# An attention and feed-forward kernel: three batch-1 transposes placed later, four start-up loads merged into two

## The chip, the cores and the metric

The kernel runs on one core of a Trainium2 chip. The metric is device time in microseconds (us). The profile covers one execution; the times come from six. Five engines are named as in the profile: PE is the matmul engine (PEld its weight loads), DVE the vector engine, ACT the scalar engine, POOL GpSimd, and SP the engine that here only issues transfers. Each runs its own instruction stream in program order and waits on the others through semaphores.

## The reference

Squared-ReLU attention over 8 batches, 12 heads, 448 tokens and 64 features a head, and then a feed-forward block on the joined heads (768 wide, 3072 inside) with a layer norm ahead of it and a residual:

```python
scores = scale * np.matmul(q, k.transpose(0, 1, 3, 2))
attn = np.maximum(scores, 0.0) ** 2 / S
x = np.matmul(attn, v)                       # heads joined: (8, 448, 768)
...
xn = (x - mu) / np.sqrt(var + 1e-06) * g_ln
out = x + np.maximum(xn @ w_ch1, 0.0) @ w_ch2
```

## The kernel before

**Units.** Heads go in pairs: a batch has six, and pair i is pair i % 6 of batch i // 6, so pairs 0 to 5 are batch 0, 6 to 11 batch 1, 12 to 17 batch 2. A pair's scores are made by `att_QK` in four tiles of keys (three of 128 keys, and the last 64 keys, which two pairs share), ReLU is done by ACT or DVE on the way out of PSUM, DVE squares in `att_square`, and `att_AV` multiplies with v and writes the transposed x (`xT_of(b, pair)`) as bf16.

**Two ways of getting q and k transposed.** Pairs 0 to 11 are loaded whole into `early` (`load_heads`) and transposed on PE against an identity (`pe_T`, line 235). From pair 12 on, `load_qk` fills one of three slots of `qk_ring` by three loads on POOL's queue (lines 174 to 176), and `att_T` issues one DMA transpose of that slot on SP's queue (line 259) into one of three `qkT` buffers. So the transpose of pair 16 needs the load of pair 16 landed, and the buffer of pair 13 read for the last time; its landing frees the slot for the load of pair 19.

**Batch 0.** Its attention runs alone at the start (`step_fine`, `first_end`), fed by loads whose order is written out by hand in the last part of the kernel. All loads that cast float32 to bf16 go through POOL's queue in program order: batch 0's heads, batch 1's, the first weights `w1` in six pieces, the second weights `w2` in four, and then pairs 12 to 14. Batch 0's q and k came in groups of heads 2-3, 4-5, 6-7 and 8-11 (heads 0 and 1 through two other queues). The v of heads 0 to 3 and the last 64 rows of all v stood between the groups 4-5 and 6-7.

**From then on a batch's first feed-forward product carries the next batch's attention.** `ffn_1_all(b)` walks over 24 column tiles ni of 128; each is 12 matmuls at line 446 and one ReLU on ACT. At chosen ni (`IN_SECOND` = 3, 6, 9, 13, 15, 18, 21 for b = 1) an `excursion` puts three score tiles of the next batch in between; when it holds a pair's last tile, `queued` issues the transpose of the pair three further on and notes the load six further on, which goes out at the next excursion. The order in batch 1 is: ni = 3: pair 12, first three tiles; ni = 6: pair 12's last tile, pair 13 (then the transpose of 15 is issued); ni = 9: pair 13's third tile, pair 14 (transpose of 16); ni = 13 (transpose of 17); ni = 15: two tiles of pair 15 and the first of pair 16, whose halves go to spare PSUM banks and are cleared by ACT and DVE.

**The residual and the statistics.** `ffn_x(b, ki)` transposes one of six 128-feature pieces of x to token order by a DMA transpose on SP's queue (line 423) into `x_tok`. For batch 1 pieces 0 to 2 go out during batch 0's second product and pieces 3 to 5 in `ffn_1_all(1)`. `ffn_stats` (lines 437 to 439, DVE, two bn_stats and one bn_aggr) reads a 128-token tile of all six pieces; `STATS_AT[b]` gives the ni at which the four tiles of the batch are done. The results are used in `ffn_rstd`, after the last ni.

Of the kernel before, what the change touches and what calls it, by code (L numbers as in the profile page):

```python
# [11 lines left out]
def kernel(  # L12
# [17 lines left out]
    B, H, S, D = q.shape  # L30
# [108 lines left out]
    def v_parts(b):  # L139
        v_sb = v1_sb if b == 1 else v_ring  # L140
        return (v_sb[:, :H * NF * D].rearrange("p (h e) -> p h e", h=H),
                v_sb[:, H * NF * D:].rearrange("p (a e) -> p a e", a=NPAIR))

    def load_heads(b, pieces):
        v_heads, v_rest = v_parts(b)
        for name, h0, hs in pieces:
            heads = slice(h0, h0 + hs)
            if name == "q":
                nc.gpsimd.dma_start(first_q[b][:, heads].rearrange("p h j d -> p h (j d)"),  # L149
                                    q[b, heads].rearrange("h (p j) d -> p h (j d)", j=NJ))  # L150
            elif name == "k":
                nc.gpsimd.dma_start(first_k[b][:, heads, :NF].rearrange("p h t d -> p h (t d)"),  # L152
                                    k[b, heads, :SF].rearrange("h (p t) d -> p h (t d)", t=NF))
            elif name == "k last":
                nc.gpsimd.dma_start(first_k[b][:SS, heads, NF], k[b, heads, SF:].rearrange("h s d -> s h d"))
            elif name == "v":
                nc.gpsimd.dma_start(v_heads[:, heads], v[b, heads, :SF].rearrange("h (p t) d -> p h (t d)", t=NF))
            elif name == "v last":
                for e in range(4):
                    r0 = row0(e // 2, e % 2)  # L160
                    nc.gpsimd.dma_start(v_rest[r0:r0 + SS, e // 2::2, r0:r0 + D],
                                        v[b, e::4, SF:].rearrange("g s d -> s g d"))

    def row0(i, hh):

        return D * ((i + hh) % 2)
# [246 lines left out]
    def tiles_of(b):  # L413
        return range(b * S // P, (b + 1) * S // P)
# [10 lines left out]
    def x_carry(b):  # L425

        nc.scalar.copy(xT[:, :, :D], x_first[:, :, S - D:] if b == 0 else xT[:, :, S:])
# [291 lines left out]
    def flush_loads():  # L719
        while loads:  # L720
            load_qk(loads.pop(0))
# [103 lines left out]
    def ffn_1_first():  # L825
        f_ps, m_ps = next_f(), next_f()
        tiles = [t[:, :S] for t in (f_ps, m_ps, spare[1], next_sc()[:, 0])]
        for ki in range(K1):
            if ki < GAIN_FIRST:
                center_part(ki, mean0)  # L830
            else:
                nc.vector.tensor_tensor(xc[:, ki, :], mean0, xT_of(0, ki), op=Alu.add)
                nc.scalar.activation(xc[:, ki, :], xc[:, ki, :], Act.Identity, scale=g_sb[:, ki:ki + 1])
            for ni, ps in enumerate(tiles):
                nc.tensor.matmul(ps, w1[:, ki, ni * P:(ni + 1) * P], xc[:, ki, :],
                                 start=(ki == 0), stop=(ki == K1 - 1))
        for ni, ps in enumerate(tiles):
            nc.scalar.activation(h[:, ni, CARRY:], ps, Act.Relu)
        for t in range(2):
            att_square(NPAIR, t)  # L840
        excursion(1)
# [4 lines left out]
    T_IN_FIRST = {10: 3, 13: 4, 16: 5}  # L846
    X_AT = (9, 10, 11, 12, 13, 14)
    V_AT = {22: PE_T * NPAIR + 2, 23: PE_T * NPAIR + 4}
    STATS_AT = {0: (18, 21, 23), 1: (14, 16, 19, 22), 2: (2, 5, 8, 14), 3: (2, 5, 8, 11)}
    IN_SECOND = (3, 6, 9, 13, 15, 18, 21)  # L850
    IN_REST = (1, 3, 6, 9, 12, 15, 18)
    X_SUMS_AT = {0: (0, 1, 2), 4: (3,), 7: (4,)}
# [1 line left out]
    def ffn_1_all(b):  # L854
        ms = tiles_of(b)
        units = () if b < UNIT_FROM else (UNIT,) if b < B - 1 else (*LAST_UNITS, UNIT)
        for ni in range(NI0 if b == 0 else 0, units[0] if units else K2):
            if b == 0 and ni == NI0:
                ffn_1_first()
            if b == 0 and ni == NI0 + 2:  # L860
                x_carry(0)
            if b == 0 and ni == X_AT[0]:

                nc.sync.dma_start(held, h[:1, ni - 1, CARRY:CARRY + 16])
            if b == 0 and ni in X_AT:
                ffn_x(b, X_AT.index(ni))
            if b == 0 and ni == IN_FIRST[-1] + 1:
                flush_loads()
            if b == 0 and ni in V_AT:
                load_v(V_AT[ni])  # L870
            bursts = (IN_FIRST, IN_SECOND, IN_REST)[min(b, 2)]

            late = ni == 0 and b > 1 and b * S // (2 * P) - (b - 1) * S // (2 * P) == 1
            ffn_1(ni, spare[1] if late or b < B - 1 and ni in bursts and len(ready) > 1 else None)
            flush()
            at = STATS_AT[min(b, 2) if b < B - 1 else 3][:len(ms)]
            if ni in at:
                ffn_stats(ms[at.index(ni)])
            if b >= UNIT_FROM:
                for n in X_SUMS_AT.get(ni, ()):  # L880
                    x_sum(n)
            if b == 1:
                for n, part in enumerate(p for p, at in zip(LATE_SUMS, SUMS_AT) if at == ni):
                    if ni == REST_AT and n < 2:
                        ffn_2_first_rest(n)
                    w2_sums(*part)
            if b == 0:
                if ni in IN_FIRST:
                    excursion(3)
                if ni == IN_FIRST[-1] + 3:  # L890
                    next_AV(bank=spare[1])
                if ni in T_IN_FIRST:
                    att_T(NPAIR + T_IN_FIRST[ni])
            elif b < B - 1:
                if ni in bursts:
                    first = nc.vector if b > 1 and ni == bursts[0] else nc.scalar
                    excursion(3, third=(first, nc.vector), **(dict(evac_by=nc.scalar) if b == 1 else {}))
                    if b == 1 and ni == bursts[1]:
                        for ki in range(X_FIRST, K1):
                            ffn_x(1, ki)  # L900
                    while ni > bursts[3] and held_stores:
                        held_stores.pop(0)()
                if b == 1 and ni == K2 - 1:
                    flush_loads()
                    next_AV(bank=spare[1])

        late = []

        def between(n):
            if n == 2:  # L910
                flush_loads()
            if n == 3:
                next_AV(bank=sc_turn.items[0][:, 0], evac_by=nc.scalar, later=late)
            if n == 5:
                posts.extend(late)


        f0, f1 = f_turn.items
        if b == B - 1:
            unit(units[0], (f0, spare[1], spare[0], f1), accs[0], accs[2])  # L920
            unit(units[1], (f1, f0, spare[1], spare[0]), accs[3], accs[4])
            unit(units[2], (spare[0], f1, f0, spare[1]), accs[0], accs[2])
        elif units:
            unit(UNIT, (f0, spare[1], spare[0], f1), accs[0], accs[1], between)
# [84 lines left out]
    with tc.manual_schedule(engines=set(ENGINES)):  # L1009
        load_early()  # L1010
        load_heads(0, [("q", 2, 2), ("k", 2, 2)])
        make_identity(nc, identity)
        load_heads(0, [("k last", 0, 4), ("q", 4, 2), ("k", 4, 2), ("k last", 4, 4), ("v", 0, 4),
                       ("v last", 0, H), ("q", 6, 2), ("k", 6, 2), ("q", 8, 4), ("k", 8, 4),
                       ("k last", 8, 4), ("v", 4, 4), ("v", 8, 4)])
        load_heads(1, [("q", 0, 2), ("k", 0, 2), ("k last", 0, H)])
        load_heads(1, [("q", 2, 4), ("k", 2, 4)])
        load_w1(0)
        load_w1(1)
        load_w1(2)  # L1020
        load_heads(1, [("q", 6, 6), ("k", 6, 6), ("v", 0, H), ("v last", 0, H)])
        for c in range(3, NCH):
            load_w1(c)
        warm_up(20)
        att_T(0)
        warm_up(2)
        for i in range(0, NPAIR, 2):
            step_fine(i)
        first_end()
        load_w2(B11, 0, 0)  # L1030
        load_w2(B21, 1, 0)
        load_w2(B12, 0, 1)
        load_w2(B22, 1, 1)
        nc.gpsimd.memset(qk_ring, 0.0)
        i = PE_T * NPAIR
        load_qk(i)
        load_qk(i + 1)
        load_qk(i + 2)
        load_v(i)
        for b in range(B):  # L1040
            ffn_1_all(b)
            if b == 0:
                ffn_2_first()
            else:
                ffn_2_all(b)
        flush()
# [30 lines left out]
```

## Time and profile before

| | |
|---|---|
| median of 6 runs | 518.68 us (517.47 to 519.88) |
| the profiled execution | 519.27 us, span 517.5 us |
| PE busy | 508.9 us, 98% of the span |
| DVE, ACT, POOL busy | 403.1, 287.3, 225.7 us |
| PE clock granted | full over the span |
| share of the chain that ended last | PE 80%, DMA 14%, POOL 4% |
| POOL's transfer queue | 25.75 MB |

The span is what the profiler saw of the program; the execution's own time is 1.8 us more. PE is busy nearly throughout, so the time of the kernel is PE's work and the few moments when PE waits. A wait of PE is printed in its timeline in square brackets behind the instruction that it precedes, with what ended it.

### The profile page before, as it was taken

The numbers are of one execution on the slowest core, as the hardware profiler recorded it, in microseconds if no ns is written. First come the engines' busy times: TensorE is split into PE (matmuls) and PEld (weight loads), VectorE is DVE, ScalarE is ACT, GpSimd is POOL, SyncE is SP. The second block draws the span as 40 slices with busy tenths as digits, with TensorE's granted clock in tenths as the row PEclk, the third lists the DMA queues.
The fourth block names the chain that finished last, engine by engine and source line by source line (L and its number), as shares of the span: only waits on it lengthen the run. The fifth ranks groups of instructions, "written<-read, shape, count | busy, mean of one in ns | idle before, by whom it ended". The sixth has DMA issues, their size and how long they took to land.

```text
span 517.5 us, 14362 instructions
## 1 busy us (share of the span) xinstructions
PE 508.9 (98%) x5979; PEld 321.6 (62%) x5979; DVE 403.1 (78%) x720; ACT 287.3 (56%) x487; POOL 225.7 (44%) x259
## 2 busy tenths in 40 slices
PE   8899999999999999999999999999999999999996
PEld 4345566546875576655766557655766557667865
DVE  5866779969988779687785868987896869993855
ACT  6887551777238772387723876487624876234220
POOL 9817113967732863228532376337632000330031
PEclk9999999999999999999999999999999999999999
DMA  9999999999636991559924599469934300250022
GB/s 114 174 202 198 183 204 159 142 154 183 82 83 103 117 107 49 124 75 131 92 52 109 80 123 140 81 81 112 83 69 111 65 1 3 72 114 3 1 60 64
DMA packets 175312, 53.05 MB, mean 103 GB/s; under 512 B 154256, under 2 KB 175248, under 8 KB 175248
## 3 DMA queue, kind: packets, MB, share of 16 engines
q0 software_dynamic: 103744, 25.75, 55.7%
q1 hardware_dynamic: 70976, 26.03, 26.8%
q8 instruction: 46, 0.75, 0.6%
q10 hardware_dynamic: 528, 0.37, 0.2%
q14 instruction: 18, 0.15, 0.1%
HBM read 51.91 MB, written 11.01 MB: 122 GB/s over the span
## 4 chain that ended last, share of the span: by engine, by line
PE 80%; DMA 14%; POOL 4%; issue 1%; ACT 1%; DVE 0%; SPq 0%; POOLq 0%
PE f L521 34%; PE f L446 29%; PE f L672 6%; DMA qk_ring<-in_k_dram 6%; DMA s_sb<-in_v_dram 4%; PE f L330 4%; PE sc L300 3%; DMA qkT_t<-qk_ring 2%; PE f L300 1%; DMA w<-in_k_dram 1%; PE sc L295 1%; PE sc L330 1%; POOL w L152 1%; PE f L353 1%; POOL w L213 1%; POOL w L149 1%
## 5 line engine op out<-in xcount | busy, mean ns | idle before, releaser
L446 PE MATMUL f<-xc,w 128*64 128x448 bf16 x1872 | 189.0, 354 | 0.1
L446 PEld LDWEIGHTS <-w 128*64 128x64 bf16 x1872 | 105.1, 110 | 76.6 <-issue 14.4
L521 PE MATMUL f<-w,s_sb 128*64 128x384 bf16 (+2 forms) x1584 | 130.0, 324 | 0.0
L448 ACT ACTIVATE h<-f 128x448 bf16<-128x448 f32 x156 | 85.9, 551 | 65.7 <-PE f L446 60.9
L521 PEld LDWEIGHTS <-s_sb 128*64 128x64 bf16 x1584 | 92.3, 110 | 34.8
L310 ACT ACTIVATE at<-sc 128x896 bf16<-128x896 f32 x120 | 103.1, 919 | 10.1 <-PE sc L300 10.1
L313 DVE TENSOR_TENSOR at<-at 128x896 bf16<-128x896 bf16 x168 | 96.6, 620 | 6.8 <-ACT at L310 6.0
L554 POOL TENSOR_TENSOR o_t<-o_t,x_tok 128x384 f32<-128x384 f32 x26 | 25.3, 972 | 148.1 <-ACT o_t L553 148.1
L174 POOL DMA_DIRECT2D qk_ring<-in_q_dram x36 | 46.8, 1301 | 85.6 <-DMA qkT_t<-qk_ring 60.0
L553 ACT ACTIVATE o_t<-f,rstd 128x384 f32<-128x384 f32 x26 | 15.1, 581 | 95.8 <-DVE acc_t L558 37.0
L515 DVE TENSOR_TENSOR s_sb<-h 128x1536 bf16<-128x1536 bf16 x65 | 64.4, 1004 | 0.0
L175 POOL DMA_DIRECT2D qk_ring<-in_k_dram x36 | 55.9, 1554 | 10.8 <-DMA w<-in_moe_w_ch_dram 10.8
L521 PE MATMUL f<-w,h 128*64 128x384 bf16 x624 | 52.9, 326 | 0.0
L176 POOL DMA_DIRECT2D qk_ring<-in_k_dram x36 | 46.6, 1295 | 5.3 <-DMA w<-in_moe_w_ch_dram 4.8
L306 DVE TENSOR_SCALAR at<-f 128x448 bf16<-128x448 f32 x59 | 35.5, 615 | 13.8 <-PE f L300 13.8
L521 PEld LDWEIGHTS <-h 128*64 128x64 bf16 x624 | 36.5, 110 | 13.6
L554 POOL TENSOR_TENSOR acc_t<-acc_t,x_tok 128x384 f32<-128x384 f32 x24 | 28.5, 1195 | 20.0 <-ACT acc_t L553 19.9
L186 POOL DMA_DIRECT2D v_ring<-in_v_dram x36 | 33.3, 1268 | 0.0
L330 PE MATMUL f<-at,v_ring 128*64 128x448 bf16 x248 | 31.1, 357 | 0.5 <-DMA v_ring<-in_v_dram 0.5
L410 DVE SCALAR_TENSOR_TENSOR xc<-f,g_sb,xc 128x448 bf16<-128x448 f32 x45 | 28.5, 678 | 3.8 <-PE f L404 3.8
L300 PE MATMUL sc<-qkT_t 64*128 64x448 bf16 x192 | 30.0, 357 | 0.5 <-DMA qkT_t<-qk_ring 0.5
L369 DVE TENSOR_SCALAR xT<-f 128x448 bf16<-128x448 f32 x22 | 13.6, 618 | 18.9 <-ACT at L310 11.1
(130 smaller groups left out, 566.1 us busy)
## 6 DMA issues: line engine op xcount, KB each, us to landing
w<-in_moe_w_ch_dram POOLq DMA_DIRECT2D x6, 768.0 KB, 13.5
w<-in_moe_w_ch_dram POOLq DMA_DIRECT2D x4, 1152.0 KB, 29.1
v_ring<-in_v_dram POOLq DMA_DIRECT2D x21, 192.0 KB, 4.8
qk_ring<-in_q_dram POOLq DMA_DIRECT2D x36, 112.0 KB, 5.0
qk_ring<-in_k_dram POOLq DMA_DIRECT2D x36, 96.0 KB, 4.9
out_dram<-o_t SPq DMA_DIRECT2D x8, 168.0 KB, 2.2
out_dram<-acc_t SPq DMA_DIRECT2D x7, 168.0 KB, 2.2
out_dram<-o_t SPq DMA_DIRECT2D x8, 144.0 KB, 2.1
```

What stands on the lines that cost most here:

```text
L174: nc.gpsimd.dma_start(q_to, q[b, heads].rearrange("x (p j) d -> p j x d", j=NJ))
L175: nc.gpsimd.dma_start(k_to[:, :NF], k[b, heads, :SF].rearrange("x (p t) d -> p t x d", t=NF))
L176: nc.gpsimd.dma_start(k_to[:SS, NF], k[b, 2 * a:2 * a + 2, SF:].rearrange("x s d -> s x d"))
L300: nc.tensor.matmul(by_j(half[hh]), k_of(i, r, t, P), q_of(i, r), start=True, stop=True)
L310: nc.scalar.activation(at, ps[:, :, :S], Act.Relu)
L313: nc.vector.tensor_mul(attn[i, t], attn[i, t], attn[i, t])
L330: nc.tensor.matmul(ps[hh * D:(hh + 1) * D, :], weights, values, start=start, stop=stop)
L446: nc.tensor.matmul(ps[c * D:(c + 1) * D, :], w1[:, ki, n0:n0 + D], xc[:, ki, :], start=(ki == 0), stop=(ki == K1 - 1))
L448: nc.scalar.activation(h[:, ni, CARRY:], ps, Act.Relu)
L515: nc.vector.tensor_tensor(s_sb[:, n], x, y, op=op)
L521: nc.tensor.matmul(ps[c * D:(c + 1) * D, :d1 - d0], stat[:, ki, c * D:(c + 1) * D], w2[:, slot, ki, d0:d1], start=(start and ki == 0), sto ...
L554: nc.gpsimd.tensor_tensor(o_t, o_t, x_half(m, dh), op=Alu.add)
```

## The change

Three statements are edited. In batch 0's list of loads, q of heads 4 and 5 and q of heads 6 and 7 become one load at the place of the former, and likewise k. In batch 1, pieces 3 to 5 of x go out one excursion later, at ni = 9, so on SP's queue they stand behind the transpose of pair 16 instead of ahead of it; and the statistics of batch 1 stand at ni = 16, 18, 20, 22 instead of 14, 16, 19, 22.

```diff
-    STATS_AT = {0: (18, 21, 23), 1: (14, 16, 19, 22), 2: (2, 5, 8, 14), 3: (2, 5, 8, 11)}
+    STATS_AT = {0: (18, 21, 23), 1: (16, 18, 20, 22), 2: (2, 5, 8, 14), 3: (2, 5, 8, 11)}
...
-                    if b == 1 and ni == bursts[1]:
+                    if b == 1 and ni == bursts[2]:
                         for ki in range(X_FIRST, K1):
                             ffn_x(1, ki)
...
         load_heads(0, [("q", 2, 2), ("k", 2, 2)])
         make_identity(nc, identity)
-        load_heads(0, [("k last", 0, 4), ("q", 4, 2), ("k", 4, 2), ("k last", 4, 4), ("v", 0, 4),
-                       ("v last", 0, H), ("q", 6, 2), ("k", 6, 2), ("q", 8, 4), ("k", 8, 4),
-                       ("k last", 8, 4), ("v", 4, 4), ("v", 8, 4)])
+        load_heads(0, [("k last", 0, 4), ("q", 4, 4), ("k", 4, 4), ("k last", 4, 4), ("v", 0, 4),
+                       ("v last", 0, H), ("q", 8, 4), ("k", 8, 4), ("k last", 8, 4), ("v", 4, 4), ("v", 8, 4)])
```

## The prediction

> **What bounds the kernel now.** I read PE's timeline first, for its brackets: PE is busy 98% of the span, so only its waits can be won. After 1.23 us it waits five times, and never after 110.12 us. The four larger ones:
>
> ```profile
> 13.88 0.76 PE L235 MATMUL f<-identity,w 112*64 112x112 bf16 x16 [1.18 <-DMA w<-in_q_dram]
> ...
> 18.82 0.57 PE L330 MATMUL f<-at,v_ring 128*64 128x448 bf16 x4 [0.49 <-DMA v_ring<-in_v_dram]
> ...
> 90.03 0.55 PE L300 MATMUL sc<-qkT_t 64*128 64x448 bf16 x4 [0.47 <-DMA qkT_t<-qk_ring]
> ...
> 110.12 0.36 PE L300 MATMUL f<-qkT_t 64*128 64x448 bf16 x2 [0.68 <-DMA qkT_t<-qk_ring]
> ```
>
> The first is pair 3's PE transpose, late by q of heads 6 and 7. The second is pair 2's product with v. The third is pair 12, the first that comes through the ring. The fourth is the first tile of pair 16, at ni = 15. All are waits for transfers, 2.82 us together. As PE then runs on without a gap, what is won at 110 us reaches the end whole.
>
> Next the chain that ended last: it comes to 90 us not over PE but over transfers.
>
> ```profile
> 52.41 31.80 DMA qk_ring<-in_k_dram
> 84.36 5.63 DMA qkT_t<-qk_ring
> ```
>
> The last load of pair 12 lay 31.8 us in POOL's queue behind w1 and w2. So the start-up gains nothing beyond 0.47 us unless this stream of loads ends earlier too. Whether it can is in the stretches (windows; last two columns DMA share and GB/s) and in POOL's timeline:
>
> ```profile
> 4.00:9.00 5.00, 5.00 (x54) 2.88 (x52) 2.73 (x9) 2.56 (x5) 5.00 (x9) 1.00 1.25 125
> 9.00:14.00 5.00, 3.82 (x45) 1.62 (x45) 4.38 (x8) 4.71 (x6) 5.00 (x8) 1.00 1.10 108
> 14.00:24.00 10.00, 9.43 (x107) 3.85 (x107) 8.57 (x16) 8.35 (x10) 8.51 (x12) 1.00 1.59 173
> ```
>
> ```profile
> 4.03 0.67 POOL L149 DMA_DIRECT2D w<-in_q_dram  x1
> 4.69 0.73 POOL L152 DMA_DIRECT2D w<-in_k_dram  x1
> 5.41 0.64 POOL L155 DMA_DIRECT2D w<-in_k_dram  x1
> 6.02 0.78 POOL L157 DMA_DIRECT2D v_ring<-in_v_dram  x1
> 6.77 2.48 POOL L161 DMA_DIRECT2D v_ring<-in_v_dram  x4
> 9.23 0.69 POOL L149 DMA_DIRECT2D w<-in_q_dram  x1
> 9.90 0.72 POOL L152 DMA_DIRECT2D w<-in_k_dram  x1
> 10.62 0.72 POOL L149 DMA_DIRECT2D w<-in_q_dram  x1
> ```
>
> From 4 to 14 us POOL is busy the whole time and the transfers run at 125 and 108 GB/s; from 14 us on at 173. So up to 14 us POOL's issuing sets the pace, not the transfers. The lines at 9.23 and 9.90 (q and k of heads 6, 7) are those that the change drops.
>
> Last, SP's queue around pair 16, with that transpose's landing (last column of the issue list, us from issue):
>
> ```profile
> 97.60 1.23 SPq L259 DMA_TRANSPOSE qkT_t<-qk_ring  x1
> 98.89 4.26 SPq L423 DMA_TRANSPOSE x_tok<-xT  x3
> 103.33 4.33 SPq L259 DMA_TRANSPOSE qkT_t<-qk_ring  x2
> ```
>
> ```profile
> qkT_t<-qk_ring SPq DMA_TRANSPOSE x1, 6.7
> ```
>
> Pair 15's transpose, three pieces of x, then pair 16's at 103.33, landing 6.7 us later at 110.08: PE's wait to 110.12. The three pieces hold SP from 98.89 to 103.15.
>
> **The change part by part.**
>
> *Merged loads, POOL.* Two instructions go (0.69 and 0.72), and the two kept grow from 0.67 and 0.73 to the 0.72 and 0.77 of the four-head loads at 10.62 and 11.32. All behind them is issued 1.41 - 0.09 = 1.3 us earlier. POOL waits later for landings (0.38 us at 16.74, for q of heads 8 to 11), but those come earlier in step.
>
> *Merged loads, transfers.* Bytes are the same, so the stream ends earlier by the slack filled before 14 us. Bounds: 0, if service and not issue was the limit, and 1.3, the whole head start. 10 us at 117 GB/s would take 6.8 us at 173, so there are about 3 us to fill; I take 1.0. From 24 to 84 us the stretches show 190 to 201 GB/s, full, so this 1.0 arrives undiminished at pair 12's transpose: landing 89.0 instead of 89.99.
>
> *Merged loads, PE.* The wait of 1.18 goes: heads 6 and 7 are then issued with 4 and 5. What is late next is what stands behind: k of heads 4 to 7, and v of heads 0 to 3, which get 208 KB (112 and 96) more ahead of them. The Trainium skill ("DMA: Bandwidth & Descriptors", section "Anatomy of one DMA — SWDGE (gpsimd) path") puts a transfer at about 2.0 us plus bytes over 436 GB/s: as an estimate 208 KB then cost 0.5 us, v lands at 10.65 + 0.5 = 11.15, and PE, which takes it at 11.04, waits 0.1. The rows speak against that rule: q of heads 4, 5 landed 3.6 us after issue where the rule gives 2.3, and even the full stretch moves 173 GB/s: 208 KB are 1.2 us, v at 11.85, a wait of 0.8. As the transfers had slack there, I take 11.4, a wait of 0.4. The k of heads 4 to 7: the two-head load landed at 8.16, plus up to 1.2 is 9.4; pair 2's transpose at 10.11 takes it with no wait, though with 0.7 us to spare. By 13 us PE is thus 1.18 - 0.4 = 0.8 ahead (0.4 to 1.1). ACT follows: its ReLUs idle 1.26 us before 14.98 for want of that very transpose.
>
> At 18.82 the v of heads 4 to 7 ends the wait; it comes 1.0 earlier and PE 0.8, so PE is ahead by the lesser of 0.8 + 0.49 and 1.0. At 90 us: PE arrives at 89.56 - 1.0, the transpose lands at 89.0. **The win is 1.0**: the lesser of the stream's head start and PE's plus its old waits. The PE side alone would allow 1.18 + 0.49 + 0.47 - 0.4 = 1.74, so the stream decides.
>
> *x pieces behind pair 16, SP.* Pair 16's transpose needs its load (last piece landed at 99.53: issued 94.45, 5.1 us) and pair 13's last read (98.80 + 0.36). SP is free at 98.83. So it issues at about 99.6 instead of 103.33, and with 5.7 to 6.7 us lands by 105.3 to 106.3; PE wants it at 109.44. **The wait of 0.68 goes**, with 3 us to spare. ACT's ReLU of tile 16 stands behind two score tiles from 109.44 (0.91 and 0.93), so it may return a few hundredths; I take 0.65.
>
> *Who is delayed by it.* The pieces of x go out at 101 to 105.3 instead of 98.89 to 103.15 and land by about 111 (the last took 6.2 before). Pair 17's transpose, behind them, is issued at 105.85 and waits then for pair 14's last tile anyway; its data are wanted at 120. POOL's load of pair 19 no longer waits until 110.66 for the ring slot and goes 4 us earlier; nothing on POOL but loads stands behind it. Its data cross pair 17's and 18's, which have 8 us and more.
>
> *Statistics, DVE.* 0.56 + 0.55 + 0.21, 1.3 us, move from ni = 14 to 18 in effect, ahead of that excursion's DVE work (evacuating the odd pair's bank, squares). Cover there:
>
> ```profile
> 115.50 0.39 DVE L379 TENSOR_TENSOR xs<-xs,xT 128x448 bf16<-128x448 bf16 x1 [1.02 <-ACT xT L367]
> ```
>
> In exchange the 1.3 us before 111.14 are gone, so DVE reaches 115.5 with the same sum of work behind it; 1.02 and 0.40 us of idle time follow. Cost 0. Without cover it would be up to 1.3 less that idle.
>
> **Sum.** 1.0 + 0.65 = 1.65 us, so the profiled 519.27 becomes 517.6 and the median of the runs shown, 518.68, becomes 517.0. What a measurement can tell from no change is about 0.2%, 1.04 us.
>
> **Rivals.**
>
> *The stream does not move* (17%). If the dips before 14 us were service, PE meets pair 12 at 89.99 as before, and the merge gives nothing: 0.65 left, 518.0, within 0.2%. For it: the four-head load at 10.62 took 5.8 us to land where two-head ones took 3.6 to 4.6, so bytes count. Against: POOL without a pause and 108 GB/s.
>
> *Only the merge works* (8%). Pair 16 waits for something else, say its own load pushed back: 1.0, 517.7, which straddles the bound.
>
> *x lands late and DVE stands* (slower, 12%). The statistics of ni = 16 wait for the last piece. DVE then has 1.3 and 1.3 us of statistics, 0.39 of sum and 0.62 of evacuation before the bank that PE wants for ni = 20, about 116.6: landing plus 3.7. It decides from a landing at 112.9. Transposes of x in this trace landed after at most 12.5 us, beside full traffic; from 104.2 that is 116.7: 3.8 lost, 1.65 won, 520.8. Against: the same three took 6.2 to 7.1 us here, so the slack is about 2 us.
>
> That the change doesn't do what it says is excluded for SP (program order) and can be true only of loads landing in another order.
>
> **How the numbers follow.** The forecast, 1.2 to 2.0 won, 63%. Low end: 1.3 + 0.68 is the most that the rows allow, 516.7, and 0.6 for the spread of the runs: 516.1. High end: the stream that does not move, 518.0, with its spread, to 518.9; the slow case and a tail are outside. Faster by over 0.2% holds the forecast and a part of the second rival: 0.67. Within: the first rival and the rest: 0.21. Slower: 0.12.
>
> **What would show it.** PE's timeline: no bracket near 12.7 but perhaps one near 11.0 (v); the bracket near 89 there or larger, at 89.0; none near 109. POOL: q of heads 8 to 11 at 9.3. SP: a line 259 transpose at about 98.6, right behind pair 15's. DVE: no wait at ni = 16. It is wrong if pair 12's transpose still lands at 89.9 or the x pieces hold DVE.

## The result and the profile after

The kernel with the change takes 516.69 us (median of 21 runs, 515.92 to 518.19); the kernel before, run beside it on the same chips, takes 518.43 (42 runs, 516.91 to 521.5). The ratio is 0.9963 [0.9953, 0.9974], a gain of about 1.9 us (0.0037 × 518.4). The forecast was 1.65 us and 517.0. One execution of 1049.9 us, in e1 below, is left out throughout.

The two profiled executions lie further apart: 519.27 us before, 516.16 after, or 3.1 us. The one before lies 0.8 above its median and the one after 0.5 below. So the traces say where time was won, and the ratio how much.

PE's timeline of the kernel after, all rows with a bracket (start, us, engine, line, operation, tiles, count, idle time before it and what ended it; here and below, the rows between those shown are left out):

```profile
1.23 4.43 PE L713 MATMUL f<-w,ones 128*128 128x256 bf16 x20 [1.23 <-DVE w L108]
...
17.14 0.57 PE L330 MATMUL f<-at,v_ring 128*64 128x448 bf16 x4 [0.33 <-DMA v_ring<-in_v_dram]
26.28 0.70 PE L235 MATMUL f<-identity,w 112*64 112x112 bf16 x16 [0.15 <-DVE x_tok L369]
```

Of the four waits shown of before, three are gone (1.18, 0.47 and 0.68) and the 0.49 is down to 0.33 at 17.14. The same instruction starts earlier by 1.2 us at pair 3's transposes (13.88 to 12.69), 1.7 at pair 2's product with v (18.82 to 17.14), 2.2 at pair 12 (90.03 to 87.82), 3.05 at pair 16 (110.12 to 107.07), and 3.1 at the end of the span. So in this pair of profiles 2.2 of the 3.1 are won up to pair 12 and 0.85 between there and pair 16. The second figure is not the worth of the second part by itself: e7 below, with the loads alone, reaches pair 16 at 107.05.

The chain that ended last, after:

```profile
PE 93%; POOL 2%; DVE 2%; DMA 1%; ACT 1%; issue 0%; POOLq 0%
```

```profile
11.44 5.66 DMA v_ring<-in_v_dram
```

The second line is the last transfer in the chain (start, us). It ends at 17.10; from there to the end of the span the chain runs over engines alone, where before it held 31.8 us of a load and 5.63 us of pair 12's transpose.

The stretches and POOL's timeline, in the columns of the prediction:

```profile
4.00:9.00 5.00, 5.00 (x54) 2.83 (x52) 2.93 (x9) 2.61 (x5) 5.00 (x9) 1.00 1.34 147
9.00:14.00 5.00, 4.97 (x62) 2.23 (x61) 4.56 (x9) 5.00 (x7) 4.94 (x8) 1.00 1.43 144
14.00:24.00 10.00, 9.67 (x107) 3.92 (x104) 9.73 (x19) 9.65 (x12) 8.86 (x12) 1.00 1.45 186
```

```profile
4.02 0.72 POOL L149 DMA_DIRECT2D w<-in_q_dram  x1
4.72 0.76 POOL L152 DMA_DIRECT2D w<-in_k_dram  x1
...
6.08 0.78 POOL L157 DMA_DIRECT2D v_ring<-in_v_dram  x1
6.82 2.49 POOL L161 DMA_DIRECT2D v_ring<-in_v_dram  x4
9.29 0.74 POOL L149 DMA_DIRECT2D w<-in_q_dram  x1
```

The loads of heads 8 to 11 now begin at 9.29 instead of 10.62: 1.33 us of head start, as worked out. But from 4 to 14 us 1455 KB are moved instead of 1165 (the rates by 5 us each), and from 14 to 24 another 1860 instead of 1730. The stream gained more than the head start: pair 12's transpose is issued at 81.81 and landed at 87.49, 2.5 us earlier than the 89.99 of before. It comes ahead of PE, so there is no bracket.

Where the head start grows is in POOL's timeline a little later, before and then after:

```profile
16.74 0.73 POOL L149 DMA_DIRECT2D w<-in_q_dram  x1 [0.38 <-DMA w<-in_q_dram]
17.77 0.75 POOL L152 DMA_DIRECT2D w<-in_k_dram  x1 [0.30 <-DMA w<-in_k_dram]
...
23.38 1.02 POOL L157 DMA_DIRECT2D s_sb<-in_v_dram  x1 [0.81 <-DMA w<-in_k_dram]
```

```profile
20.81 1.03 POOL L157 DMA_DIRECT2D s_sb<-in_v_dram  x1
```

Before, POOL waited 0.38, 0.30 and 0.81 us for loads to land before it could issue further ones; after, these three waits are gone. The q of heads 8 to 11 lands at 14.12 instead of 16.46, 2.3 us earlier for 1.3 of earlier issue. So the v of batch 1 is issued 2.57 us earlier (20.81 for 23.38), and pair 12's transpose lands by about as much earlier.

SP's queue around pair 16, after:

```profile
94.71 3.81 SPq L259 DMA_TRANSPOSE qkT_t<-qk_ring  x2
98.57 4.43 SPq L423 DMA_TRANSPOSE x_tok<-xT  x3
103.64 1.24 SPq L259 DMA_TRANSPOSE qkT_t<-qk_ring  x1
```

The first line is pair 15's and pair 16's transpose one behind the other, then the pieces of x, then pair 17's. Pair 16's is issued at 97.29 and landed at 102.79, 4.3 us before PE wants it at 107.07.

DVE's timeline where the statistics now stand:

```profile
110.06 0.55 DVE L437 BATCH_NORM_STATS2 stats<-x_tok 128x6 f32<-128x384 bf16 x1
...
111.23 0.51 DVE L437 BATCH_NORM_STATS2 stats<-x_tok 128x6 f32<-128x384 bf16 x1
...
113.23 0.62 DVE L369 TENSOR_SCALAR xT<-f 128x448 bf16<-128x448 f32 x1 [0.40 <-PE f L330]
```

The statistics of ni = 16 and of 18 run back to back without a wait (the last piece of x had landed at 107.26), and DVE then still waits 0.40 for PE. They cost nothing.

### The profile page after: what moved, and what is told of

The parts are those of the page before. It is cut to its first block, busy times and chain, and to the rows that moved or that the text cites. A ratio compares the mean times of both kernels' runs of the same rounds, so it can differ in the third digit from the quotient of the medians.

```text
span 514.4 us, 14358 instructions
## 1 busy us (share of the span) xinstructions
PE 508.4 (99%) x5979; PEld 321.4 (62%) x5979; DVE 402.8 (78%) x720; ACT 287.2 (56%) x487; POOL 224.0 (44%) x257
## 3 DMA queue, kind: packets, MB, share of 16 engines
q0 software_dynamic: 103712, 25.75, 55.1%
HBM read 51.91 MB, written 11.01 MB: 122 GB/s over the span
## 4 chain that ended last, share of the span: by engine, by line
PE 93%; POOL 2%; DVE 2%; DMA 1%; ACT 1%; issue 0%; POOLq 0%
PE f L446 35%; PE f L521 35%; PE f L672 6%; PE f L330 5%; PE sc L300 4%; PE f L500 3%; PE f L300 2%; DMA v_ring<-in_v_dram 1%; PE sc L295 1%; PE f L353 1%; PE sc L330 1%; PE f L835 1%; DVE at L313 1%; ACT at L310 1%; POOL v_ring L161 0%; DVE x_tok L369 0%
```

## The experiments

Each kernel was timed in five rounds beside the kernel before, whose median was 518.5 to 518.6 in every set.

**e1, e7: the loads alone.** Only the diff's third part.

> The merged loads alone; the x pieces and the statistics stay as before. Theory (the load stream ends earlier and PE's start-up waits go): PE is ahead by 1.2 us at 14 us and by 2.2 us at pair 12, no bracket near 88; the bracket of pair 16, about 0.7 us, stays (near 108). Time 1.0 to 1.6 us under the kernel before, about 517.2. Rival (the stream stays where it was, PE meets pair 12 at 90.0 with a longer bracket): 0 to 0.2 us, 518.3.

> The merged loads alone once more, for a profile at full clock. By the part alone: brackets at 13.88 and 90 gone, PE 2.2 us ahead at pair 12. Whether pair 16 is still waited for is open: with the x pieces ahead of it its transpose should be issued near 100.8 and land near 107.4, and PE wants it near 107.2, so a bracket of 0 to 0.7 us. Time about 516.9 to 517.3.

e1: 516.89 us, 0.9971 [0.996, 0.9982]. e7 is the same kernel, run again for its profile: 517.1 us, 0.9971 [0.9961, 0.9982]. Both say 1.5 us. PE's timeline of e7:

```profile
11.27 0.57 PE L330 MATMUL f<-at,v_ring 128*64 128x448 bf16 x4 [0.16 <-DMA v_ring<-in_v_dram]
```

This and 0.15 us at 26.04 are all that is left after 1.23. Pair 12's transpose landed at 87.35. And there is no wait for pair 16, though the pieces of x stand ahead of its transpose as before: it landed at 107.00 and PE took it at 107.05. SP's queue had come early with the stream. So the 0.68 is no fixed cost: it is a race that PE loses in one execution and wins by hundredths in another. Of the seven profiles with the old order on SP's queue and no added transposes, two show the wait (before and e9 below) and five do not (e3, e4, e6, e7, e12).

**e2: the pieces of x and the statistics alone.** The diff's first two parts.

> The x pieces behind pair 16's transpose and the later statistics alone; the loads as before. Theory (only the bracket at 110.12 goes): brackets at 13.88, 18.82 and 90.03 stay at 1.2, 0.5 and 0.5 us, none near 109; 0.6 to 0.7 us under the kernel before, about 517.8. Rival (x lands late, DVE stands at ni = 16 and PE waits for a bank near ni = 20): a new bracket near 116 and no gain.

518.08 us, 0.9989 [0.9979, 1.0]: 0.6 us, by its interval 0 to 1.1. Profile 518.47, PE's timeline:

```profile
14.54 0.51 PE L235 MATMUL f<-identity,w 128*64 128x128 bf16 x8 [1.17 <-DMA w<-in_k_dram]
18.78 0.57 PE L330 MATMUL f<-at,v_ring 128*64 128x448 bf16 x4 [0.31 <-DMA v_ring<-in_v_dram]
90.12 0.55 PE L300 MATMUL sc<-qkT_t 64*128 64x448 bf16 x4 [0.54 <-DMA qkT_t<-qk_ring]
...
109.37 0.35 PE L300 MATMUL f<-qkT_t 64*128 64x448 bf16 x2
```

The two start-up waits shown and pair 12's are those of before, within 0.2 us; the wait for pair 16 is gone (its transpose was issued at 99.28 and landed at 105.80). That is the predicted step, by itself: 99.6 and 105.3 to 106.3 had been written.

**e5, e6: the two halves of that part.** e5 moves the pieces and leaves the statistics at 14, 16, 19, 22; e6 moves only the statistics.

> The x pieces behind pair 16's transpose, with the statistics left at ni = 14, 16, 19, 22. If the later statistics were needed, DVE waits at ni = 14 for the last piece (landing near 109.8) about 0 us before it would run there at 110 anyway, and PE shows no new bracket: time as of the two together, 518.1. Rival: DVE stands 1 us or more, the tile of pair 16 is cleared late, and PE waits near 112 to 116: no gain, 518.5 or more.

> The statistics of batch 1 at ni = 16, 18, 20, 22 alone. Theory: DVE has idle time at both places, nothing moves: 518.5, within 0.3 us. Its profile also shows once more with the loads and the order of before whether PE waits for pair 16: if that bracket of 0.68 us is a fixture it is there again; if it is a race that PE loses in some executions, it may be absent or of another length.

e5: 518.21 us, 0.9998 [0.9986, 1.001]. e6: 518.3 us, 0.9998 [0.9987, 1.0008]. Neither is told from no change. In e5's profile pair 16 is not waited for (issued 99.11, landed 106.69), and some 0.25 us go at 114.06, where pair 17 had landed at 114.02. e6's profile, PE's timeline:

```profile
13.56 0.70 PE L235 MATMUL f<-identity,w 112*64 112x112 bf16 x16 [0.87 <-DMA w<-in_q_dram]
88.62 0.55 PE L300 MATMUL sc<-qkT_t 64*128 64x448 bf16 x4 [0.27 <-DMA qkT_t<-qk_ring]
```

Here too the bracket at pair 16 is missing, with the queue as it was before: landed 107.68, taken 107.87. That the statistics must move with the pieces is neither shown nor excluded: e2 and e5 differ by 0.5 us, with overlapping intervals.

**e3: the same order, without merging.** Heads 6 and 7 in loads of their own, but behind 4 and 5, so the number of loads is that of before.

```diff
-        load_heads(0, [("k last", 0, 4), ("q", 4, 2), ("k", 4, 2), ("k last", 4, 4), ("v", 0, 4),
-                       ("v last", 0, H), ("q", 6, 2), ("k", 6, 2), ("q", 8, 4), ("k", 8, 4),
+        load_heads(0, [("k last", 0, 4), ("q", 4, 2), ("k", 4, 2), ("q", 6, 2), ("k", 6, 2), ("k last", 4, 4),
+                       ("v", 0, 4), ("v last", 0, H), ("q", 8, 4), ("k", 8, 4),
                        ("k last", 8, 4), ("v", 4, 4), ("v", 8, 4)])
```

> q and k of heads 6, 7 as loads of their own, but issued directly behind those of heads 4, 5, so early delivery without fewer issues; POOL then issues q of heads 8 to 11 at 10.6 us as before. Theory A (fewer issues give the stream its head start): the bracket at 13.88 goes, but v of heads 0 to 3 is issued at 7.4 instead of 6.1 us and PE waits about 1 us near 11; pair 12's transpose lands at 89.5 to 90; 0 to 0.5 us gained. Theory B (the order alone does it, because the transfer engines get more work early): pair 12's transpose lands by 88.5 and the gain is as of the merge, 1.0 to 1.6 us.

517.71 us, 0.9987 [0.9976, 0.9997]: 0.7 us. PE's timeline:

```profile
11.71 0.57 PE L330 MATMUL f<-at,v_ring 128*64 128x448 bf16 x4 [0.88 <-DMA v_ring<-in_v_dram]
13.60 0.38 PE L330 MATMUL f<-at,v_ring 128*64 128x448 bf16 x1 [0.52 <-DMA v_ring<-in_v_dram]
18.50 0.57 PE L330 MATMUL f<-at,v_ring 128*64 128x448 bf16 x4 [0.17 <-DMA v_ring<-in_v_dram]
```

Now it is v that is late. Its load is issued at 7.37, where the merge issues it at 6.08, and lands at 11.67 instead of 11.06, and the last rows of v follow: 1.40 us lost at the place where 1.18 are won. So early heads 6 and 7 need the merge, because without it their two issues stand ahead of v. In this one profile pair 12's transpose landed at 87.78 all the same, which is what the theory of the order alone had asked for; e6, with the loads as before, has 88.58, so one profile does not decide it.

**e4, e9: the merge without its head start.** A memset of 1.40 us on POOL, into a ring that is not yet in use, holds the queue where the dropped loads stood; it is added work. e9 adds eight dummy matmuls on PE ahead of pair 2's product with v.

```diff
+        load_heads(0, [("k last", 0, 4), ("q", 4, 4), ("k", 4, 4), ("k last", 4, 4), ("v", 0, 4),
+                       ("v last", 0, H)])
+        nc.gpsimd.memset(qk_ring.rearrange("p a j c -> p (a j c)")[:, :1536], 0.0)
+        load_heads(0, [("q", 8, 4), ("k", 8, 4), ("k last", 8, 4), ("v", 4, 4), ("v", 8, 4)])
```

The lines of e9 alone:

```diff
+        if i == 2:
+            warm_up(8)
```

> The merged loads, with a memset of half the ring put on POOL where the two loads were dropped; it takes about 1.35 us, so q of heads 8 to 11 is issued at 10.6 us as before. Theory A (the head start in issue is all): pair 12's transpose lands near 90.0 again, PE waits there 1.7 to 2.2 us, gain 0 to 0.3 us. Theory B (half of the stream's 2.5 us comes from fuller service and not from issue): it lands near 88.7, gain 0.9 to 1.3 us.

e4: 519.06 us, 1.001 [0.9991, 1.0028]. The whole gain of the merge is lost. PE's timeline and the stretches of e4:

```profile
17.50 0.22 PE L235 MATMUL f<-identity,w 64*64 64x64 bf16 x2 [0.70 <-DMA w<-in_k_dram]
...
18.89 0.57 PE L330 MATMUL f<-at,v_ring 128*64 128x448 bf16 x4 [0.88 <-DMA v_ring<-in_v_dram]
```

```profile
17.00:20.20 3.20, 1.82 (x13) 0.68 (x15) 1.93 (x4) 1.50 (x3) 2.67 (x4) 1.00 1.59 169
20.20:23.60 3.40, 3.40 (x28) 1.18 (x24) 2.31 (x4) 2.20 (x3) 3.39 (x4) 0.50 1.42 195
23.60:27.00 3.40, 3.40 (x39) 1.38 (x37) 3.00 (x6) 3.13 (x5) 1.27 (x3) 1.00 1.24 206
```

Heads 8 to 11 are issued at 10.82, and two waits of 1.58 us together come back a few microseconds later. Pair 12's transpose landed at 90.05, where it was before the change; PE does not wait for it there, as had been expected, because it comes only at 90.97 itself. The reason is something that no theory had: right behind the two waits the granted clock (third column from the end) is 0.50 for one stretch, PE does 28 matmuls in 3.4 us where the next stretch holds 39, and 1.4 us more are lost. In seven of e4's 14 executions the granted clock is 0.997 or less, as in this one, and their median is 519.6; that of the other seven is 518.0, as good as that of the kernel before in its executions with a higher clock (518.1). So without its head start the merge wins nothing, and the fallen clock makes it a loss.

e9 was made to take that away.

> The merged loads with the held-up POOL, as in the run with the memset, and eight of the start-up's idle matmuls (about 0.1 us each) ahead of pair 2's product with v, where PE waited 0.88 us there. Theory (that run lost about 1.5 us because PE's waits near 18 us let its clock fall to half from 20.2 to 23.6 us): the clock stays full, PE passes 24 us about 1.5 us earlier, the median falls from 519.1 to about 518. Rival (the clock fell for another reason, or does not matter): the median stays at 519 or goes up by the matmuls' own time.

e9: 521.02 us, 1.0046 [1.0029, 1.0063]; a fall to 518 was expected, so that expectation failed. The clock stayed at 1.00 and at 23.6 us PE was 1.3 us ahead of e4, but:

```profile
17.61 0.22 PE L235 MATMUL f<-identity,w 64*64 64x64 bf16 x2 [0.99 <-DMA w<-in_k_dram]
90.48 0.55 PE L300 MATMUL sc<-qkT_t 64*128 64x448 bf16 x4 [0.70 <-DMA qkT_t<-qk_ring]
...
111.09 0.36 PE L300 MATMUL f<-qkT_t 64*128 64x448 bf16 x2 [0.66 <-DMA qkT_t<-qk_ring]
```

At 90 us the stream takes back 0.8 of what the fuller clock had won (transpose landed at 90.43), and the waits at 106.13 (0.18) and 111.09 cost it 1.4 more. PE is then 0.9 us behind e4, up to its last matmul (514.12 for 513.23); the span ends 2.0 us later. The 1.1 between them lie in the output: the last store is issued at 516.48 instead of 514.12. At 514.06 a packet of 16 KB stands on e9's instruction queue and takes 1.49 us, while e4's last one is at 503.76. So the added instructions may cost at the end as well; that this packet held up the stores is not shown. Both kernels say that without the head start the merge leaves pair 12 where it was.

**e12: two issues fewer, but late.** Heads 6 to 11 in one load each, where 6 and 7 stood.

```diff
-                       ("v last", 0, H), ("q", 6, 2), ("k", 6, 2), ("q", 8, 4), ("k", 8, 4),
+                       ("v last", 0, H), ("q", 6, 6), ("k", 6, 6),
```

> Two loads fewer as in the change, but without early delivery: q and k of heads 4, 5 early as before, and heads 6 to 11 in one load each where heads 6, 7 stood. Theory (both halves are needed: the stream of loads gains from fewer issues, PE from early heads 6, 7): pair 12's transpose is issued near 82 as in the change, but PE waits 2 to 3 us near 13 and meets pair 12 at 89.5 to 90.5 without a bracket; gain 0 to 0.5 us. Rival (PE's start-up waits do not matter, only the stream): as the merge, 1.3 to 1.7 us gained.

521.6 us, 1.0064 [1.0039, 1.0089]: 3.3 us slower, where 0 to 0.5 gained had been expected. PE's timeline and stretches:

```profile
15.31 0.39 PE L235 MATMUL f<-identity,w 112*64 112x112 bf16 x8 [2.40 <-DMA w<-in_q_dram]
16.84 0.69 PE L235 MATMUL f<-identity,w 128*64 128x128 bf16 x8 [1.15 <-DMA w<-in_k_dram]
```

```profile
12.00:17.00 5.00, 1.45 (x20) 0.64 (x20) 2.02 (x4) 1.92 (x3) 3.93 (x6) 0.99 1.55 184
17.00:20.30 3.30, 3.30 (x24) 0.90 (x20) 1.78 (x3) 1.78 (x2) 3.22 (x5) 0.50 1.68 185
```

POOL's issues are as few as in the merge, and pair 12's transpose landed at 88.62, earlier than before; but pair 3 waits for six heads instead of two, the clock halves behind that, and PE comes to pair 12 only at 92.76. The larger load is itself part of that wait, so this is no clean test of late delivery; but with e4 it fits that what the merge wins it wins with both: heads 6 and 7 early, and the head start.

**e10, e11: SP's order, with the suspected cost doubled.** Three more transposes of x, whose output is used by nobody, behind the three that there are: in the place of before (e10), and in that of the change, whose other parts are in as well (e11).

```diff
         for ki in range(X_FIRST, K1):
             ffn_x(1, ki)
+        for ki in range(X_FIRST, K1):
+            nc.sync.dma_start_transpose(x_tok[:, 4:7, ki * P:(ki + 1) * P], xT[:, ki, :3 * P])
```

> The kernel before with three more DMA transposes of x (into slots that are free then, their data unused) behind the three pieces, so six stand ahead of pair 16's transpose on SP's queue. Theory (each piece ahead costs 1.3 to 1.4 us of SP and moves pair 16's landing by as much, and PE waits for it): pair 16's transpose is issued near 107 and PE waits 3.5 to 4.7 us for its tile at ni = 15; time 3 to 4.5 us over the kernel before. Rival (SP's order does not decide the landing, the transfer engines do): under 1.5 us.

524.16 us, 1.01 [1.008, 1.0121]: 5.2 us slower by the ratio, where 3 to 4.5 had been expected. SP's queue and PE's timeline of e10:

```profile
99.72 4.00 SPq L423 DMA_TRANSPOSE x_tok<-xT  x3
103.81 3.87 SPq L902 DMA_TRANSPOSE x_tok<-xT  x3
107.85 3.34 SPq L259 DMA_TRANSPOSE qkT_t<-qk_ring  x2
```

```profile
113.95 0.36 PE L300 MATMUL f<-qkT_t 64*128 64x448 bf16 x2 [3.82 <-DMA qkT_t<-qk_ring]
```

Three more transposes hold SP for 3.87 us, pair 16's is issued 4.5 us later, and PE waits 3.82 instead of 0.68. Up to there the kernel differs from the one before in nothing but what stands ahead of that transpose in SP's queue. From 114.8 to 118.2 us the granted clock is again 0.50, which adds 1.7 us to that wait; the expectation had left it out.

> The changed kernel with the same three more transposes, all six behind pair 16's. Theory: pair 16 is not waited for; pair 17's transpose slips to about 108 and is wanted at 117.6, so PE waits for nothing new: 516.7, within 0.5 us of the changed kernel. Rival (the statistics or pair 17 become late): 1 us or more over it.

520.07 us, 1.0037 [1.0024, 1.005], 3.2 us over the 516.84 of the changed kernel beside it (e8). Pair 16, now ahead of all six, landed at 104.46 and is not waited for. But no new wait had been expected, and there is one:

```profile
114.92 0.38 PE L295 MATMUL sc<-qkT_t 64*64 64x448 bf16 x2 [1.87 <-DMA qkT_t<-qk_ring]
```

This is the tile of last keys that pair 16 shares with pair 17. It needs pair 17's transpose, which stood behind the six pieces: issued at 108.03, landed at 114.88. In the changed kernel that transpose lands at 109.64 and is wanted at about 111.7, so the room behind pair 16 is 2 us. The 1.87 is not all of the loss: in ten of the 22 executions the granted clock is 0.997 or less (median 521.4), and in the others the median is 519.5.

**e8: the changed kernel once more.**

> The changed kernel once more, for its distance to the merged loads alone on the same footing: ratio 0.9963 again, about 516.7; if the x pieces are worth nothing on top of the merge, 0.997. Its profile should show no bracket near 88 or 107, PE being about 3 us ahead of the profile before.

516.84 us, 0.9958 [0.9943, 0.9973]. In its profile, 516.48, pair 12's transpose landed at 88.07 and there is one bracket at the stream, which had not been expected:

```profile
88.11 0.55 PE L300 MATMUL sc<-qkT_t 64*128 64x448 bf16 x4 [0.40 <-DMA qkT_t<-qk_ring]
```

So which of the two comes last at pair 12, PE or the stream, changes from one execution to the next, and the 87.49 of the first profile is on the early side.

## Why the prediction was right, point by point

The time held: 1.65 us forecast, 1.9 measured, most of it from the loads. Within the intervals the parts add up: 1.5 (e1, e7) and 0.6 (e2) against 1.9. That the sum came so close is in part luck, since the first term was too small (1.0 for 1.5) and the second rather too large (0.65; on top of the loads it is 1.9 - 1.5 = 0.4, not told from nothing). By its own steps:

*POOL issues 1.3 earlier.* Right: 9.29 for 10.62.

*The stream gains 1.0, at most 1.3.* This is the mis-sized term, and its upper bound was false. Pair 12's transpose landed at 87.35, 87.49, 88.07 and 88.82 in the four profiles with the merge and its head start (e7, after, e8, e11), and from 88.58 (e6) to 90.68 (e10) in the five with the loads as before: 1.9 us earlier by the means, with a spread between executions that is as large. The head start itself is needed: with POOL held up, pair 12 was at 90.05 and 90.43. The step that failed is "those come earlier in step": POOL's later waits for landings did not move with the loads, they fell away. In the profile of before they are 0.38, 0.30 and 0.81 us up to 24 us, while POOL stands once for 0.2 to 0.3 in each of after, e7 and e8. With the loads as before their length changes with the execution (none at all in e6, the earliest of the five). And the transpose lands late or early with the bytes moved from 4 to 24 us: 3.3 MB in after, e7 and e8; 3.1 in e6, e11, e12 and e3, which landed at 87.8 to 88.8; 2.9 to 3.0 in all that landed at 89.9 or later. Why the same loads are served faster in one execution than in another stays open.

*PE: the 1.18 goes, v costs 0.4.* The first held. The v of heads 0 to 3 landed at 11.06 in the profile after, 0.41 us later than the 10.65 of before; over the other profiles it is more: 10.05 to 10.65 with the old loads ahead of it (six with before, mean 10.40) and 11.06 to 11.98 with the 208 KB more (six, mean 11.33), so 0.9. PE waited less than 0.1 for it in the profile after, 0.16 in e7, 0.42 in e11. The rows of the full stretch had given 1.2 and the rule of the Trainium skill ("DMA: Bandwidth & Descriptors", section "Anatomy of one DMA — SWDGE (gpsimd) path") 0.5. But these are bytes as written, in bf16. The profile counts 51.91 MB read from HBM, twice the 25.75 of POOL's queue; counted by what is read, 416 KB, the rule's estimate is 1.0, close to the 0.9. As a duration for one whole transfer the rule was short again: the four-head q took 4.76 us from issue (4.02) to landing (8.78), where about 2.0 us and 224 KB over 436 GB/s make 2.5, and 448 KB 3.1.

*The win of the merge is 1.0, "the stream decides".* Too small: 1.5 by two ratios. In the profiles after and e7 PE came last at pair 12, in e8 and e11 the stream did, with 0.40 and 0.27; so the stream does not always decide. And one term had been put at nothing, the clock ("full over the span", in the one profile). The record has the granted clock of every execution. In the sets of the experiments it is 0.997 or less in 49 of the 138 executions of the kernel before, and their median is 519.0 us; that of the other 89 is 518.1. With the merge it is so low in 2 of 48 (e1, e7, e8). Leaving these out on both sides, the loads alone take 517.0, and their gain is 1.1 by the medians and 1.3 by the means, as much as the bound allowed. The other 0.3 or so (49/138 of 0.9) goes with the clock falling less often. It is an upper figure for the clock itself, since longer waits both cost time and come ahead of such falls; the last section has when it falls.

*The 0.68 goes.* The mechanism is shown by e10 and e2. What failed is the premise that 0.68 is a fixture: five profiles had the old queue and no such wait. So 0.65 is what the profile of before lost there, and the part's worth in the mean is e2's 0.6, which its interval doesn't part from nothing. On top of the merge, 0.9963 and 0.9958 against 0.9971 lean the right way, with overlapping intervals.

*Pair 17 is wanted at 120.* Wrong. The shared tile of last keys wants it at about 114.7 in the trace of before; e11 found it. It cost nothing, since 2 us of room were enough for three pieces.

*Statistics at no cost.* Right, as DVE's rows show. The slower rival (x late, DVE stands) had room to spare: the last piece landed at 107.26. The limit of 112.9 was reckoned in the times of before; with PE 3 us ahead it is about 109.9.

*The rivals with a smaller gain.* The stream does move, by 1.9 us as above, so the first falls. Of "only the merge works" the reason falls: pair 16's transpose was held up by nothing else, and is issued at 97.29. Its outcome is not excluded, since the whole change and the loads alone are not told apart in time.

## What to carry to other kernels

When the start is paced by one queue's issuing, two small loads fewer ahead of everything can be worth more than the wait that they end; but only if what the merged load brings is wanted early, and only after asking what now stands behind it (here v, with almost nothing to spare). A short wait seen in one profile is often a race between two streams: look at a second execution before putting its length into a sum. The same holds for a clock that is full in one profile. And when a transfer is moved back in a queue, look for the first user of whatever it passes, a shared last tile included, not for the loop step that bears its name.

## What was not expected of the hardware

After PE had waited, its granted clock fell to 0.50 for one stretch of 3.41 us: in e4 after 0.70 and 0.88 us, in e12 after 2.40 and 1.15, in e10 after 3.82 and, in the start-up, after 1.45. It cost 1.4 us in e4 and 1.7 in e10's later place, in e4 nearly as much as the waits themselves.

The traces give the times of these falls. The full clock had stood for 10.24 us before e12's and e10's first, 13.65 before e4's and 95.57 before e10's second: 3, 3, 4 and 28 times 3.41. So the clock seems to be set once per window of 3.41 us. In the window that ended with a fall PE was busy for 14% (e12), 25% and 58% (e10) and 54% (e4) of the time. In every other window, counted from the start of the full clock in thirteen profiles up to 125 us, it was busy for 63% or more: 63% at e5's wait of 1.25 us, 70% at the 1.18 of before. So in these profiles the busy share of one window parts the falls from the rest, somewhere between 58 and 63%, and the length of one wait does not. The windows do not start at a fixed time (the full clock begins at 4.8 to 7.1 us; until then the matmuls run at about half pace, those of line 713 beginning 0.21 us apart instead of 0.12), so the same wait can fall into one window or be shared by two. That would explain why the kernel before loses the clock in some executions and not in others; of those only the profiled one shows its windows.

The Trainium skill ("TensorE: Matmul & The Clock Gate", section "🔬 Part 1: The HAM clock gate (the "warmup" mystery)") tells of such a gate, with windows of 3413 ns, and its table has the half clock after at least one idle window. The length and the half agree with these rows, but a window without any work was not needed here. e9's dummy matmuls, which filled the gap, kept the clock at 0.998 or more in all eight executions, where e4 lost it in seven of 14. So a wait at the start can cost more than its bracket.
